# Attention and a gated two-layer network on one core: all of w_in converted before w_out, fewer weight loads queued ahead of the transposes of P, and a new plan

## The chip, the cores and the metric

The kernel runs on one core of a Trainium2 chip. The metric is the device time of one execution in microseconds (us). Before the change the median of three executions was 715.66 us (714.78 to 718.32).

## The reference, cut to what matters

```
q, k, v: (4 batches, 8 heads, 1152, 64)      x: (2304, 512)
q_pool = q.reshape(B, H, 576, 2, D).mean(axis=3)
scores = q_pool @ k.T / sqrt(D);  attn = softmax(scores);  out = attn @ v
x = out.transpose(0, 2, 1, 3).reshape(B * 576, H * D)
h = x @ w_in          # 512 x 2048
g = h * sigmoid(h)
result = g @ w_out    # 2048 x 512
```

The result is float32. All matrix products except the first scores are done as three products of float16 halves (a high part and the rest): high by high, high by low, low by high. The weights come from the host as 64-bit floats, so one weight is eight bytes, and the kernel makes the two float16 parts of each itself.

## The kernel before, in words

**Work.** The 32 heads are 16 pairs, four pairs to a batch. A job (`job`, line 731) is 128 pooled query rows of one pair: the scores S of both heads (`scores`, L723), the row maximum on VectorE (DVE, L784 and L791), the exponential on ScalarE (ACT, L800), then P cut into a high part (L816, recorded at helper lines 408 or 412) and a low part (L820, recorded at L432, mostly on GpSimd, POOL). Both parts are transposed by a DMA that SyncE (SP) issues (L827, tile `pt`), and TensorE (PE) multiplies them with V (`finish`, L935, tile `po`). In the first four jobs one of the two sides is transposed by PE instead (L841, tile `pp`). `guard` (L755) adds a small constant to the row sums and, after a reciprocal, L1007 scales `po` into x. There are 72 jobs: 64 of 128 rows of one pair, and 8 that hold the left-over 64 rows of two pairs.

**The network.** When the four jobs of 128 rows of a batch are finished, `rows` (L1017) turns x around, on PE for the first two blocks (L1064) and by DMA after that (L1044), and `block` (L1104) runs the two layers: `first(u)` for four quarters u (L1130, 48 products each, tile `mm`), tanh, gate, and the two parts of g (tile `g`, at most ten live at once by `MOST`, four to a block); then `second` (L1225, 48 products of 512 columns), which for the first block is cut into four pieces and for the second block into two (`PIECES`), each needing only a part of w_out. Quarter u of the first layer needs only the eighths 2u and 2u+1 of w_in.

**The weights.** `weights(n)` (L550) handles one of 32 pieces: an eighth u of w_in (`w1`) or w_out (`w2`), half i. It is one DMA of 512 KB (L595) and then a chain of five or six element-wise operations of 128 x 512: an ACT pass into a PSUM bank of the pool that `mm`, `po` and `pp` also use, which has two (L606); a shift on ACT or DVE (L613, L619); the two joined on DVE (L634); for w_in alone a scaling pass ("more"); the high part (`whi`); the rest (`wlo`, mostly POOL). Before, the pieces go u by u, w_in and w_out in turn:

```
        def weights(n):
            u, which, i = n // 4, n // 2 % 2, n % 2
```

The first 16 land in the space in which the second halves of the converted weights will stand later, the other 16 in the pool `b` (13 tiles in the plan), which also holds P, its parts, its transposes and the loaded q and v.

**The order.** Nothing is scheduled on the chip. `Plan.order` (L178) simulates five engines on the host with a table of costs and picks, whenever an engine is free, the ready operation of lowest priority number; the order that comes out is emitted as the program of each engine, and each engine then takes its own instructions in that order, waiting on semaphores. SP takes every load, store and transpose in one such order. Before, `departs` (L208) keeps the planner from having more than a weight of seven in flight on the DMA queue, where a transpose counts two and any other transfer one (`FLIGHT`). Priorities are sums of a job's or piece's number and a constant per kind of operation (`PRI`, `PRE` for jobs under 8, `W` for the weights, `EV` for what drains the network's products).

Of the kernel before, what the change touches and what calls it, by code (L numbers as in the profile page):

```python
# [36 lines left out]
P = 128  # L37
# [15 lines left out]

WAIT = 0.189
AHEAD, SWITCH, STEAL = 1.286, 21.317, 1.144
PREP_LEAD = 4.079
FIRST_LEAD, FIRST_STEP = 1.344, 4.504
W_FIRST, W_STEP, W2_LATER = 3.473, 0.361, -0.214
V_LATER, V_FIRST = 13.621, -45.048
PRI = dict(  # L60
    score=-258.189, top=-1.612, exp=-1.381, hi=1.631, lo=-0.034, turn=5.489, flip=13904.244,
    flat=-10.33, sums=-96.591, rows=-493.286, side=-0.32, load=-5.565, raw=0.83, xturn=-5.782,
)
PRE = dict(
    score=-0.266, top=0.223, exp=2.744, hi=1.295, lo=-1.698, turn=-0.57, sums=1.5, side=-0.268,
)
W = dict(
    t=0.374, low=0.166, put=-3777.77, more=0.289, hi=0.49, lo=-0.918,
)
EV = dict(  # L70
    x=7.188, xh=-27.052, xl=8.244, px=28.106, tanh=8.054, gate=12.388, ghi=-31.135, glo=6.951,
    osb=6.624,
)
# [16 lines left out]
FILL = {"turn": 2.79, "load": 4.6, "raw": 3.85, "store": 1.41}  # L90
MOVE = {"turn": 1.15, "load": 1.58, "raw": 1.23, "store": 0.6}
AFTER_TURN, LANDING = 0.71, 0.55
FETCH, FETCH_TIME, FETCH_STALL = 128, 1.26, 0.6
LOADS_BY, RAW_BY = "dma", "dma"
# [3 lines left out]
MORE_BY = "act", "dve", "pool"  # L98
LOW_BY = "act", "dve"
MORE = True  # L100
SUM_BY_PE = False
VC = D + 2 if SUM_BY_PE else D
X_BY_PE = 2
SIDES32 = 0
LAST = B * FULL + B // 2 - 1

# [34 lines left out]
class Plan:  # L141
# [7 lines left out]
    def add(self, options, priority, reads=(), writes=(), tiles=(), port=True, moves=None, matmuls=0, mode=0, spare=False):  # L149
        tiles = [x for t in tiles for x in (t, t.share) if x is not None]  # L150
        op = Op(options, priority, tiles, port, moves, matmuls, mode, spare)
        before = []
# [18 lines left out]
    def ready_at(self, op, engine):  # L171
        at = 0.0
        for b in op.before:
            same = b.engine == engine and engine not in ("dve", "dma")
            at = max(at, b.end + (0.0 if same else LATENCY[b.engine]))
        return at + (DMA_START if engine == "dma" else 0.0)

    def order(self):  # L178

        engines = ("pe", "dve", "act", "pool", "dma")  # L180
        free = dict.fromkeys([*engines, "port"], 0.0)
        ring, matmuls = {"dma": 0.0, "act": 0.0}, 0
        last, mode = None, 0
        flying = []
        waiting = {e: [] for e in engines}
# [21 lines left out]

        def departs(now, weight):  # L208

            landings = sorted(x for x in flying if x[0] > now)  # L210
            total = weight + sum(w for _, w in landings)
            for at, w in landings:
                if total <= FLIGHT[2] + 1e-9:
                    break
                total -= w
                now = at
            return now

        warm, used, busy, until = False, 0.0, 0.0, WINDOW
# [9 lines left out]
        def pick(e, now):  # L229
            for item in waiting[e]:  # L230
# [29 lines left out]
        while todo:  # L260
# [11 lines left out]
            while moved:  # L272
                moved = False
                for e in engines:
# [25 lines left out]
                    if op.moves:  # L300
                        what = op.moves
                        least = MOVE[what]
                        weight = FLIGHT[0] if what == "turn" else FLIGHT[1]
                        leaves = now
                        if e == "dma":
                            leaves = departs(now, weight)
                            free[e] = leaves + cost
                            if last == "turn" and what not in ("turn", "store"):
                                least += AFTER_TURN
                            last = what  # L310
                        ring[e] = max(leaves + FILL[what], ring[e] + least)
                        if e == "act" and ring["dma"] > now:
                            ring["dma"] += least
                        op.end = ring[e] + LANDING
                        if e == "dma":
                            flying = [x for x in flying if x[0] > leaves] + [(op.end, weight)]
# [44 lines left out]
def tile_kernel(tc, q, k, v, w_in, w_out, out):  # L361
    nc = tc.nc
    with ExitStack() as ctx:
# [186 lines left out]
        def weights(n):  # L550
            u, which, i = n // 4, n // 2 % 2, n % 2
            name, src, scale = (("w1", w_in, W_IN_SCALE), ("w2", w_out, W_OUT_SCALE))[which]
# [3 lines left out]
            w = wt[name, u // 4]  # L556
            if n < 16:
                space, at = n // 4, n % 4
                if at == 0:
                    wide[space] = tile("w", f"w{space % 2 + 1}_1", [P, 4, 1024], F32, "wide")  # L560
# [10 lines left out]
            t = tile("psM", "mm", [P, 512], F32)  # L571
            c = slice(i * 512, i * 512 + 512)
# [9 lines left out]

            def tu():
                return t().bitcast(U32)

            def value():
                return words(1)

            def hi():
# [7 lines left out]
                ),  # L597
                pr + PRI["raw"], writes=[("raw", *tok)], tiles=[raw], moves="raw",
            )
# [4 lines left out]
            add(  # L604
                "act", act_cost(512, True) + 0.06,
                lambda: nc.scalar.activation(  # L606
                    out=t(), in_=value(), func=AF.Prelu, scale=2.0**-111, alpha=-(2.0**32)
                ),
                pr + W["t"], [("raw", *tok)], [("t", *tok)], [t, raw], port=False,
            )  # L610
# [7 lines left out]
            def low_on(engine):  # L618
# [6 lines left out]
                "act": ("act", act_cost(512) + 0.02, low_act),  # L625
                "dve": ("dve", dve_cost(512, True), low_on(nc.vector)),
            }
            either(
                [ways[x] for x in LOW_BY],
                pr + W["low"], writes=[("low", *tok)], reads=[("raw", *tok)], tiles=[raw],  # L630
            )
            add(
                "dve", slow,
                lambda: nc.vector.scalar_tensor_tensor(  # L634
                    out=words(1).bitcast(U32), in0=tu(), scalar=3, in1=words(0).bitcast(U32),
                    op0=ALU.logical_shift_left, op1=ALU.bitwise_or,
                ),
                pr + W["put"], [("low", *tok), ("t", *tok)], [("raw", *tok)], [t, raw], port=False,
            )
            more = scale / 2.0**8  # L640
            staged = [] if n < 16 else [
                x for a in range(4) for what in ("w1", "w2") for x in weight_tokens(what, a)
            ]
# [10 lines left out]
            if more != 1.0:  # L654
                add(
                    "dve", slow,
                    lambda: nc.vector.scalar_tensor_tensor(
                        out=w()[:, u % 4, 1, c], in0=value(), scalar=more, in1=hi(),
                        op0=ALU.mult, op1=ALU.subtract,
                    ),  # L660
                    pr + W["lo"], [("raw", *tok), ("whi", *tok)], [("wlo", *tok)], [raw, w],
# [69 lines left out]
        def job(j):  # L731
# [22 lines left out]

            def guard():  # L755
                for i in range(2):
                    moves = [(slice(0, P), slice(0, P))]
# [8 lines left out]
            if SUM_BY_PE:  # L766
                return
            add(
                "dve", 0.13 if ch is not None else 0.2, guard,
                j + 0.5, [("p32", j, 0), ("p32", j, 1)], [("r", j)], [sm, r], port=False,  # L770
# [170 lines left out]
        def finish(j):  # L941
# [15 lines left out]
            for i, (pp, col) in enumerate(sides(j)):  # L957
# [7 lines left out]
                if by_32(j, i):  # L965
                    add(
                        "pe", 9 * 4 * pe_cost(64) + 0.1,
                        lambda pt=pt, pp=pp, hs=hs, keep=keep: heads(
# [363 lines left out]
```

## Time and profile before

| | |
|---|---|
| median of three executions | 715.66 us |
| the profiled execution | 714.45 us |
| its span, first to last instruction | 712.5 us |
| PE busy | 653.3 us (92%) |
| ACT, DVE, POOL busy | 480.4, 471.9, 463.9 us (67, 66, 65%) |
| mean granted PE clock | 0.976 of full |

Busy times are sums over instructions of one engine; the page's second part cuts the span into 40 slices and gives the busy share of each in tenths. PE's slices are at 4 to 8 in the first seven (about 125 us) and at 8 or 9 from there to the end.

### The profile page before, as it was taken

How to read it: one execution, taken by the hardware profiler on the slowest of the kernel's cores; microseconds unless marked ns; L12 is line 12 of the kernel's file. 1: busy time of each engine (PE TensorE's matmuls, PEld its weight loads, DVE VectorE, ACT ScalarE, POOL GpSimd, SP SyncE). 2: the span in 40 equal slices, each digit the busy share in tenths (PEclk: the TensorE clock that was granted, in tenths of full speed). 3: DMA queues.
4: the chain of work that ended last, by engine and by line, in shares of the span. 5: the costliest groups of instructions: out<-in, count | busy, mean ns of one | idle time of the engine just before them, and what ended most of it. 6: DMA issues, size and time to landing. Idle time of an engine off the chain costs nothing. (4 is left out here: it accounts for less than half of the span.)

```text
span 712.5 us, 23295 instructions
## 1 busy us (share of the span) xinstructions
PE 653.3 (92%) x10052; PEld 470.7 (66%) x10052; DVE 471.9 (66%) x839; ACT 480.4 (67%) x707; POOL 463.9 (65%) x260
## 2 busy tenths in 40 slices
PE   4656877999899999999899999998999999999997
PEld 2333655676767686767486868585868686858767
DVE  5878885689678575776678756586777565754111
ACT  4978977997577665777655766695777675865221
POOL 1657985897437776778635867887579776666111
PEclk8788999999999999999999999999999999999999
DMA  8999899999999999999999999999999999999000
GB/s 347 358 283 246 159 205 225 238 195 212 200 303 177 163 182 168 161 247 194 207 255 172 180 181 166 167 252 176 280 218 172 184 173 157 159 175 158 24 16 16
DMA packets 362886, 138.10 MB, mean 194 GB/s; under 512 B 350112, under 2 KB 350368, under 8 KB 362784
## 3 DMA queue, kind: packets, MB, share of 16 engines
q1 hardware_dynamic: 362624, 136.49, 99.6%
q8 instruction: 78, 1.28, 0.7%
q14 instruction: 24, 0.20, 0.1%
q10 hardware_dynamic: 160, 0.13, 0.1%
HBM read 45.09 MB, written 4.72 MB: 70 GB/s over the span
## 5 line engine op out<-in xcount | busy, mean ns | idle before, releaser
L432 POOL TENSOR_TENSOR phl<-p,phl 128x1152 f16<-128x1152 f32 x119 | 291.6, 2457 | 100.6 <-DVE phl L412 58.6
L800 ACT ACTIVATE p<-S,nm 128x1152 f32<-128x1152 f32 x144 | 174.8, 1215 | 99.1 <-DVE nm L791 46.5
L784 DVE TENSOR_REDUCE nm<-S 128x1 f32<-128x1152 f32 x144 | 194.5, 1351 | 53.2 <-PE S L723 52.9
L1130 PE MATMUL mm<-xt,w 128*128 128x128 f16 x3456 | 203.6, 220 | 4.8 <-DVE raw L634 2.1
L1130 PEld LDWEIGHTS <-w 128*128 128x128 f16 x3456 | 195.5, 98 | 11.1 <-DMA xt<-xs 2.5
L1225 PE MATMUL mm<-w,g 128*128 128x512 f16 x816 | 186.5, 380 | 2.1 <-DVE nm L791 1.9
L432 POOL TENSOR_TENSOR g<-t,g 128x512 f16<-128x512 f32 x72 | 98.4, 1368 | 80.4 <-ACT g L408 79.6
L723 PE MATMUL S<-K,Q 64*128 64x512 f16 (+7 forms) x1320 | 138.2, 373 | 13.4 <-ACT p L800 6.7
L935 PE MATMUL po<-V,pt 128*128 128x64 f16 (+1 forms) x4320 | 130.8, 195 | 20.0 <-DMA pt<-phl 9.8
L935 PEld LDWEIGHTS <-pt 128*128 128x128 f16 (+1 forms) x4320 | 122.3, 102 | 32.4 <-issue 12.7
L1225 PEld LDWEIGHTS <-g 128*128 128x128 f16 x816 | 75.9, 98 | 85.7 <-issue 2.5
L408 ACT ACTIVATE phl<-p 128x1152 f16<-128x1152 f32 x99 | 114.4, 1160 | 8.2 <-DMA pt<-phl 5.8
L1151 DVE SCALAR_TENSOR_TENSOR t<-t,mm 128x512 f32<-128x512 f32 x72 | 49.3, 684 | 59.8 <-ACT t L1144 57.6
L723 PEld LDWEIGHTS <-Q 64*128 64x128 f16 (+1 forms) x1080 | 42.2, 97 | 51.3 <-issue 11.1
L1144 ACT ACTIVATE t<-mm 128x512 f32<-128x512 f32 x72 | 42.5, 591 | 23.0 <-PE mm L1130 22.7
L408 ACT ACTIVATE g<-t 128x512 f16<-128x512 f32 x72 | 45.1, 627 | 18.0 <-DVE t L1151 17.9
L761 DVE TENSOR_SCALAR r<-sum 128x1 f32<-128x1 f32 (+1 forms) x152 | 17.1, 147 | 50.5 <-ACT p L800 50.1
L723 PEld LDWEIGHTS S<-K,Q 64*128 64x128 f32 (+1 forms) x240 | 23.2, 211 | 39.4 <-issue 24.2
L412 DVE CAST phl<-p 128x1152 f16<-128x1152 f32 x41 | 33.7, 822 | 9.9 <-DMA pt<-phl 7.1
L432 POOL TENSOR_TENSOR xs<-x,xs 128x512 f16<-128x512 f32 (+1 forms) x16 | 19.8, 1238 | 24.3 <-ACT xs L408 24.1
L432 DVE TENSOR_TENSOR phl<-p,phl 128x1152 f16<-128x1152 f32 x21 | 32.1, 1533 | 4.4 <-ACT phl L408 4.2
L535 DVE SCALAR_TENSOR_TENSOR V<-ld,V 128x1152 f16<-128x1152 f32 x16 | 27.6, 1729 | 6.6 <-ACT V L408 6.6
(59 smaller groups left out, 390.7 us busy)
## 6 DMA issues: line engine op xcount, KB each, us to landing
ld<-q SPq DMA_DIRECT2D x16, 576.0 KB, 5.7
ld<-v SPq DMA_DIRECT2D x16, 576.0 KB, 6.1
ld<-k SPq DMA_DIRECT2D x12, 576.0 KB, 6.4
pt<-phl SPq DMA_TRANSPOSE x280, 4.3
wide<-w_in SPq DMA_DIRECT2D x8, 512.0 KB, 8.8
wide<-w_out SPq DMA_DIRECT2D x8, 512.0 KB, 7.9
raw<-w_in SPq DMA_DIRECT2D x8, 512.0 KB, 4.9
raw<-w_out SPq DMA_DIRECT2D x8, 512.0 KB, 5.4
```

The source lines that it names most:

```text
L408: nc.scalar.activation(out=out(), in_=src(), func=AF.Copy, scale=scale or 1.0)
L412: nc.vector.tensor_copy(out=out(), in_=src())
L432: return lambda: getattr(engine, op)(out=out(), in0=a(), in1=b())
L535: lambda: nc.vector.scalar_tensor_tensor(out=values(1), in0=v3(), scalar=V_SCALE, in1=values(0)[:, :, :D], op0=ALU.mult, op1=ALU.subtract,),
L723: nc.tensor.matmul(o[to, c], lhsT=a[rows, s], rhs=x[rows, c], start=n == 0, stop=n == len(terms) - 1,)
L784: lambda: nc.vector.tensor_reduce(out=nm(), in_=ps()[:, :S], op=ALU.max, axis=AX.X),
L800: lambda: nc.scalar.activation(out=p32(), in_=ps()[:, :S], func=AF.Exp, scale=0.0625, bias=nm(), **({} if SUM_BY_PE else dict(accum_out=sm ...
L935: nc.tensor.matmul(o[to, keep : keep + n], lhsT=pt[:, hl * NK + c, cols], rhs=vv[:, at : at + n], start=c == 0 and hl + vl == 0, stop=c == ...
L1130: nc.tensor.matmul(o, lhsT=w[:, f // 2 % 4, wl, cols], rhs=moving(xl, kk), start=kk == 0 and wl + xl == 0, stop=kk == 3 and wl == 1,)
L1144: lambda: nc.scalar.activation(out=t(), in_=h(), func=AF.Tanh, scale=1.0 / G_SCALE),
L1151: lambda: nc.vector.scalar_tensor_tensor(out=t(), in0=t(), scalar=1.0, in1=h(), op0=ALU.add, op1=ALU.mult,),
L1225: nc.tensor.matmul(o(), lhsT=g[ff // 4]()[:, gl, ff % 4], rhs=w[:, u % 4, wl, e * DM : e * DM + DM], start=ff == ffs[0] and gl + wl == 0, ...
```

## The change

It does the following.

- The pieces of the weights are numbered w_in first: pieces 0 to 15 are w_in, 16 to 31 are w_out. Pieces 0 to 11 land in the space of the second halves of the converted weights or of the first half of w_out (`W_SPACES`); pieces 12 to 31, 20 instead of 16, in the pool `b`.
- In the planner `departs` and the surcharge on a load that follows a transpose are gone. Instead a weights' load is not issued while the modelled DMA queue has more than `PACE`, 5.929 us, ahead of it; a transpose holds SP's modelled queue until 0.45 us (`BACKLOG`) before the end of the transpose ahead; whatever needs a transpose is counted as ready 1.035 us (`LATE`) later than its landing; and the model of instruction fetches has other constants.
- `guard` uses one instruction for both columns of the row sums instead of two, in the 64 jobs of one pair.
- All priorities are new numbers; the plan is made anew with them.

```diff
-WAIT = 0.189
...
+WAIT = 0.233
+LATE = 1.035
...
+PREP_LEAD = 30.776
+FIRST_LEAD, FIRST_STEP = 184.155, 28.662
+W_FIRST, W_STEP, W2_LATER = -31.903, 46.348, 59.093
...
+    score=-7689049.805, top=543.78, exp=-18.862, hi=114.106, lo=-26.359, turn=1066.129,
+    flip=-951468825.963, flat=-18364455.845, sums=55234.608, rows=19917862327.894, side=-0.254,
+    load=-102.918, raw=136.844, xturn=-1240322.091,
...
+    score=-167313.439, top=-11346.633, exp=-219437.434, hi=-119435.312, lo=-264122.869,
+    turn=-755.959, sums=224665.654, side=-77.155,
...
+    t=-81.792, low=37.245, put=-86252358.206, more=34375.197, hi=-273.73, lo=164.882,
...
+W_SPACES = ("w2", 0), ("w1", 1), ("w2", 1)
...
-FLIGHT = 2, 1, 7
+BACKLOG = 0.45
+PACE = 5.929
...
-            at = max(at, b.end + (0.0 if same else LATENCY[b.engine]))
+            at = max(at, b.end + (0.0 if same else LATENCY[b.engine]) + (LATE if b.moves == "turn" else 0.0))
...
+                if e == "dma" and op.moves == "raw" and ring["dma"] > now + PACE + 1e-9:
+                    heapq.heappush(events, ring["dma"] - PACE)
+                    continue
...
+                        if what == "turn":
+                            free[e] = max(op.end, turned - BACKLOG)
+                            turned = ring[e]
...
-            u, which, i = n // 4, n // 2 % 2, n % 2
+            which, u, i = n // 16, n % 16 // 2, n % 2
...
-            if n < 16:
-                space, at = n // 4, n % 4
+            if n < 4 * len(W_SPACES):
+                space, at = W_SPACES[n // 4], n % 4
...
+                if ch is not None and by_32(j, 0) == by_32(j, 1):
+                    nc.vector.tensor_scalar(
+                        out=r(), in0=sm(), scalar1=SUM_GUARD,
+                        scalar2=1.0 / V_SCALE if by_32(j, 0) else 1.0, op0=ALU.add, op1=ALU.mult,
+                    )
+                    return
```

## Rows read from the trace of the kernel before

**Rows 1.** Windows by stage: stretch, its length, busy us (instructions) per engine, clock, DMA.
```profile
0.00:60.00 60.00, 32.83 (x270) 20.56 (x270) 44.56 (x80) 44.45 (x72) 28.32 (x25) 0.83 1.03 330
60.00:140.00 80.00, 63.95 (x886) 44.18 (x884) 59.33 (x110) 68.46 (x108) 65.35 (x41) 0.94 1.04 205
140.00:300.00 160.00, 155.64 (x2499) 113.69 (x2498) 118.36 (x203) 112.34 (x164) 108.53 (x59) 0.99 1.10 198
300.00:400.00 100.00, 94.61 (x1531) 66.78 (x1530) 72.81 (x123) 68.59 (x97) 64.36 (x35) 1.00 1.09 211
400.00:650.00 250.00, 247.38 (x4096) 179.45 (x4091) 168.06 (x311) 171.58 (x245) 181.53 (x92) 1.00 1.10 188
650.00:712.50 62.50, 58.94 (x789) 46.01 (x785) 8.83 (x14) 14.96 (x26) 15.75 (x13) 1.00 0.18 34
```

**Rows 2.** PE's waits from 0 to 140 us: us in total, times, longest.
```profile
PE pp L841 <- ACT p L800: 12.6, 4, 4.5
PE S L723 <- DMA K<-k: 6.3, 1, 6.3
PE po L935 <- DVE wide L634: 5.8, 2, 4.0
...
PE po L935 <- DMA pt<-phl: 2.0, 3, 1.0
```

**Rows 3.** PE's waits from 140 to 650 us.
```profile
PE po L935 <- DMA pt<-phl: 7.8, 13, 1.9
```

**Rows 4.** Timeline of PE: start us, us, what, count [idle before].
```profile
6.28 4.21 PE L723 MATMUL S<-K,Q 64*128 64x512 f32 x12 [6.28 <-DMA K<-k]
...
64.98 1.11 PE L1064 MATMUL px<-one,x 128*128 128x128 f32 x4 [1.84 <-DVE nm L791]
67.25 4.21 PE L723 MATMUL S<-K,Q 64*128 64x512 f32 x12 [1.15 <-ACT p L800]
...
73.14 2.85 PE L1130 MATMUL mm<-xt,w 128*128 128x128 f16 x48
75.99 2.21 PE L723 MATMUL S<-K,Q 64*128 64x512 f32 x12
...
84.41 2.21 PE L723 MATMUL S<-K,Q 64*128 64x512 f32 x12
...
92.16 2.21 PE L723 MATMUL S<-K,Q 64*128 64x512 f32 x12 [0.34 <-ACT p L800]
...
122.48 3.75 PE L723 MATMUL S<-K,Q 64*128 64x512 f32 x12 [2.20 <-ACT p L800]
```

**Rows 5.** The chain that ended last, its later part: start us, us, what.
```profile
571.37 1.68 PE po L935 x54
...
666.66 10.72 PE mm L1130 x192
677.38 10.36 PE mm L1225 x48
```

**Rows 6.** Busy DVE of line 634 alone, by stretch (the join, once per piece).
```profile
0.00:60.00 60.00, 7.58 (x12) 0.83 1.03 330
60.00:90.00 30.00, 5.01 (x8) 0.89 0.86 174
90.00:110.00 20.00, 1.96 (x3) 1.00 1.19 205
```

**Rows 7.** Timeline of SP: start us, us, what, count.
```profile
16.97 8.61 SPq L827 DMA_TRANSPOSE pt<-phl  x2
...
29.46 9.91 SPq L827 DMA_TRANSPOSE pt<-phl  x2
...
59.11 28.00 SPq L827 DMA_TRANSPOSE pt<-phl  x14
```

**Rows 8.** DMA of the first 60 us: GB/s in 40 slices of 1.5 us.
```profile
GB/s 0 166 399 412 418 412 421 418 424 414 323 366 404 426 415 421 268 297 163 384 390 379 393 363 393 186 255 154 208 369 374 372 135 348 219 390 421 393 346 154
```

**Rows 9.** Timeline of DVE: the guard, and the small operation nearest to it.
```profile
83.95 0.22 DVE L761 TENSOR_SCALAR r<-sum 128x1 f32<-128x1 f32 x2 [0.54 <-ACT p L800]
...
89.15 0.15 DVE L791 TENSOR_SCALAR nm<-nm 128x1 f32<-128x1 f32 x1
```

More of the change, by code (lines that the diff above doesn't have):

```diff
@@ L52 @@
 SUM_GUARD = 1e-9 * math.exp(P_SHIFT)
-WAIT = 0.189
[L55 to L59, printed above, removed]
+WAIT = 0.233
+LATE = 1.035
+AHEAD, SWITCH, STEAL = 1.191, 7500.906, 1.327
+PREP_LEAD = 30.776
+FIRST_LEAD, FIRST_STEP = 184.155, 28.662
+W_FIRST, W_STEP, W2_LATER = -31.903, 46.348, 59.093
+V_LATER, V_FIRST = 46260304.092, 1589936.167
 PRI = dict(
-    score=-258.189, top=-1.612, exp=-1.381, hi=1.631, lo=-0.034, turn=5.489, flip=13904.244,
-    flat=-10.33, sums=-96.591, rows=-493.286, side=-0.32, load=-5.565, raw=0.83, xturn=-5.782,
+    score=-7689049.805, top=543.78, exp=-18.862, hi=114.106, lo=-26.359, turn=1066.129,
+    flip=-951468825.963, flat=-18364455.845, sums=55234.608, rows=19917862327.894, side=-0.254,
+    load=-102.918, raw=136.844, xturn=-1240322.091,
 )
 PRE = dict(
-    score=-0.266, top=0.223, exp=2.744, hi=1.295, lo=-1.698, turn=-0.57, sums=1.5, side=-0.268,
+    score=-167313.439, top=-11346.633, exp=-219437.434, hi=-119435.312, lo=-264122.869,
+    turn=-755.959, sums=224665.654, side=-77.155,
 )
 W = dict(
-    t=0.374, low=0.166, put=-3777.77, more=0.289, hi=0.49, lo=-0.918,
+    t=-81.792, low=37.245, put=-86252358.206, more=34375.197, hi=-273.73, lo=164.882,
 )
 EV = dict(
-    x=7.188, xh=-27.052, xl=8.244, px=28.106, tanh=8.054, gate=12.388, ghi=-31.135, glo=6.951,
-    osb=6.624,
+    x=-1472.346, xh=-1738.434, xl=-56965.629, px=237092.365, tanh=-2495660.136, gate=4.509,
+    ghi=-15152.425, glo=-436.176, osb=-84.597,
 )
@@ L89 @@
 ISSUE = {"turn": 1.38, "load": 0.6, "raw": 0.6, "store": 0.6}
[L90 to L93, printed above, removed]
+FILL = {"turn": 2.87, "load": 4.23, "raw": 3.76, "store": 1.39}
+MOVE = {"turn": 0.99, "load": 1.45, "raw": 1.34, "store": 0.7}
+LANDING = 0.55
+FETCH, FETCH_LEAD, FETCH_TIME, FETCH_STALL = 128, 28, 1.24, 1.58
 LOADS_BY, RAW_BY = "dma", "dma"
@@ L150, in add @@
         tiles = [x for t in tiles for x in (t, t.share) if x is not None]
-        op = Op(options, priority, tiles, port, moves, matmuls, mode, spare)
+        op = Op(options, round(priority, 4), tiles, port, moves, matmuls, mode, spare)
         before = []
@@ L181, in order @@
         free = dict.fromkeys([*engines, "port"], 0.0)
-        ring, matmuls = {"dma": 0.0, "act": 0.0}, 0
-        last, mode = None, 0
-        flying = []
+        ring, matmuls = {"dma": 0.0, "act": 0.0}, FETCH_LEAD
+        turned, mode = 0.0, 0
         waiting = {e: [] for e in engines}
@@ L206, in shared @@
             return e == "pool" or (e == "dve" and op.port)
[L208 to L217, printed above, removed]
         warm, used, busy, until = False, 0.0, 0.0, WINDOW
@@ L301, in order @@
                         what = op.moves
[L302 to L311, printed above, removed]
+                        ring[e] = max(now + FILL[what], ring[e] + MOVE[what])
                         if e == "act" and ring["dma"] > now:
-                            ring["dma"] += least
+                            ring["dma"] += MOVE[what]
+                        if what == "turn":
+                            free[e] = max(op.end, turned - BACKLOG)
+                            turned = ring[e]
                         op.end = ring[e] + LANDING
-                        if e == "dma":
-                            flying = [x for x in flying if x[0] > leaves] + [(op.end, weight)]
                         heapq.heappush(events, free[e])
@@ L569, in bits @@
                     return raw()[:, :1024]
-            t = tile("psM", "mm", [P, 512], F32)
+            t = tile("psM", "mm", [P, 512], F32) if T_IN_PSUM else None
+            scratch = [t] if T_IN_PSUM else []
             c = slice(i * 512, i * 512 + 512)
@@ L597, in weights @@
                 ),
-                pr + PRI["raw"], writes=[("raw", *tok)], tiles=[raw], moves="raw",
+                pr + PRI["raw"], writes=[("raw", *tok), ("came", *tok)], tiles=[raw], moves="raw",
             )
             add(
-                "act", act_cost(512, True) + 0.06,
+                "act", act_cost(512, True) + 0.06 if T_IN_PSUM else 0.68,
                 lambda: nc.scalar.activation(
-                    out=t(), in_=value(), func=AF.Prelu, scale=2.0**-111, alpha=-(2.0**32)
+                    out=carried(), in_=value(), func=AF.Prelu, scale=2.0**-111, alpha=-(2.0**32)
                 ),
-                pr + W["t"], [("raw", *tok)], [("t", *tok)], [t, raw], port=False,
+                pr + W["t"], [("raw", *tok)] if T_IN_PSUM else [], [("t", *tok)] if T_IN_PSUM else [("raw", *tok), ("t", *tok)],
+                [*scratch, raw], port=False,
             )
@@ L629, in weights @@
                 [ways[x] for x in LOW_BY],
-                pr + W["low"], writes=[("low", *tok)], reads=[("raw", *tok)], tiles=[raw],
+                pr + W["low"], writes=[("low", *tok)], reads=[("raw", *tok) if T_IN_PSUM else ("came", *tok)], tiles=[raw],
             )
@@ L634, in weights @@
                 lambda: nc.vector.scalar_tensor_tensor(
-                    out=words(1).bitcast(U32), in0=tu(), scalar=3, in1=words(0).bitcast(U32),
+                    out=words(1).bitcast(U32), in0=carried().bitcast(U32), scalar=3, in1=words(0).bitcast(U32),
                     op0=ALU.logical_shift_left, op1=ALU.bitwise_or,
                 ),
-                pr + W["put"], [("low", *tok), ("t", *tok)], [("raw", *tok)], [t, raw], port=False,
+                pr + W["put"], [("low", *tok), ("t", *tok)], [("raw", *tok)], [*scratch, raw], port=not T_IN_PSUM,
             )
             more = scale / 2.0**8
-            staged = [] if n < 16 else [
-                x for a in range(4) for what in ("w1", "w2") for x in weight_tokens(what, a)
+            staged = [
+                (x, "w1", m // 2, m % 2) for at, space in enumerate(W_SPACES) if space == (name, u // 4)
+                for m in range(4 * at, 4 * at + 4) for x in ("whi", "wlo")
             ]
@@ L654, in weights, with lo_on @@
             if more != 1.0:
-                add(
-                    "dve", slow,
-                    lambda: nc.vector.scalar_tensor_tensor(
+                def lo_on(engine):
+                    return lambda: engine.scalar_tensor_tensor(
                         out=w()[:, u % 4, 1, c], in0=value(), scalar=more, in1=hi(),
                         op0=ALU.mult, op1=ALU.subtract,
-                    ),
+                    )
+                either(
+                    [x for x in (("dve", slow + 1.0, lo_on(nc.vector)), ("pool", pool_cost(512), lo_on(nc.gpsimd))) if x[0] in LO_BY],
                     pr + W["lo"], [("raw", *tok), ("whi", *tok)], [("wlo", *tok)], [raw, w],
@@ L768, in job @@
             add(
-                "dve", 0.13 if ch is not None else 0.2, guard,
+                "dve", 0.07 if ch is not None else 0.2, guard,
                 j + 0.5, [("p32", j, 0), ("p32", j, 1)], [("r", j)], [sm, r], port=False,
```

13 lines of the change are left out of this document (8 added, 5 removed).

## The prediction, made before the kernel was run

> **What bounds the kernel now.** I read the windows by stage first, because one share of busy time for the whole span hides that the limits differ. [rows 1] give PE 32.83 us busy of the first 60, 63.95 of the next 80, then 155.64 of 160, 94.61 of 100, 247.38 of 250 and 58.94 of 62.5. So PE is idle 27.2 + 16.05 = 43.2 us before 140 us and 15.9 us in the 572 us after it (4.4 + 5.4 + 2.6 + 3.6). From 140 us on the kernel is bound by PE; only the first fifth has anything large to give. The same rows show a granted clock of 0.83 and 0.94 in the first two stretches: one and the same group of twelve score products takes 4.21 us at the lower of PE's two levels, 1.2 GHz, and 2.21 us at 2.4 GHz [rows 4]; the slow groups came at the start and after stretches in which PE was mostly waiting.
>
> What holds PE in the first fifth? PE's waits there [rows 2] name the exponential of the first four jobs (12.6 us, for the transposes on PE), the first load (6.3 us) and a PSUM bank that the weights' conversion holds (5.8 us). The transposes of P by DMA stand in that list with 2.0 us only. Behind the list stand the element-wise engines: in the first 140 us DVE, ACT and POOL are busy 103.9, 112.9 and 93.7 us, 310.5 of 420 or 74%; in the second stretch 59.3, 68.5 and 65.4 of 80, with ACT at 86% [rows 1]. They convert weights and do softmax at once, so a job's scores come every 9.77 us on average over the first eight steps (84.41 - 6.28, over 8), where the step from 84.41 to 92.16 took 7.75 [rows 4]. x of the first four jobs is there only at 64.98 and the network begins at 73.14 [rows 4]; from 6 to 73 us PE has attention alone.
>
> **Part by part.** The sum is made against the profiled execution, 714.45 us; the median shown is 1.21 us above it.
>
> 1. *Attention ahead of the weights in the first eight jobs.* The new priorities put the exponential, the two parts of P and the maximum of jobs under 8 ten thousand or more below those of the conversions, the join (L634) excepted; before, conversions and jobs alternated. If the first four steps take 8.05 us, near the quickest ones seen, instead of 9.77, x of the first block and the network behind it come 4 x 1.72 = 6.9 us earlier. The conversions not done meanwhile are done later, where ACT is already at 86%, so not all of it stays. The ends are 6.9 us gained and 3 lost (the conversions of the first 60 us, twelve joins in [rows 6], pushed out by half of the 6.9 us); I take 5 us gained, because POOL is idle 31.7 of the first 60 us and DVE and ACT 15 each [rows 1].
>
> 2. *w_in first.* A block's first layer is 10.72 us of PE, its second 10.36 [rows 5]. Twelve joins were done by 60 us, 20 by 90, 23 by 110 [rows 6]. In turn order 20 pieces are five eighths of both matrices, and quarter 3 of the first layer waits for pieces 28 and 29, after 110 us. With w_in first, 16 pieces, done at about 75 us at the same pace, free all four quarters of block 0 and of block 1 as soon as its x stands; w_out begins at pieces 16 to 19, done at about 90 us, which is what the first piece of block 0's second layer needs. So some 21 us of PE work can lie between 65 and 110 us where now a quarter at a time is released. Idle there is part of the 16.05 us of the second stretch. Ends: 0 (the element-wise engines, 80% busy on average there, set the pace whatever is released) and 12 (three quarters of the idle time); I take 6. A fuller PE also meets fewer slow groups: the two at 67.25 and 122.48 us cost 2.0 and 1.5 us more than the quick one [rows 4], and I take 2 of these 3.5, with 0 and 3.5 as ends.
>
> 3. *The turns of P.* SP held two transposes for 8.61 us at 16.97 behind seven loads and for 9.91 at 29.46 behind seven, against 28.00 for fourteen, 2.0 each, at 59.11 where nothing lay ahead [rows 7]: 4.6 and 5.9 us too much. 5.929 us of modelled queue are four loads of weights at the new table's 1.34, not seven, so about three sevenths of that goes. It is hidden in the first fifth but for the 2.0 us of [rows 2]; it brings `po`, and so x, earlier, which is in 1. Later, PE waits 7.8 us for transposes in 13 places [rows 3]. The added 1.035 us makes the planner put other products in front; the longest of those waits is 1.9, the mean 0.6. Ends: 9.8 gained (all), 5 lost (an order whose other products are themselves late; half of what is there now). I take 3 gained.
>
> 4. *The guard.* Two instructions took 0.22 us, a single one on a column 0.15 [rows 9], so 0.07 less in each of 64 jobs, 4.5 us of DVE. DVE is 66% busy and behind PE after 140 us, so this is hidden by PE's products; thirteen jobs lie before, where it might show: 0 to 0.9, I take 0.5. Were PE no longer the cover, the 4.5 would count.
>
> 5. *Against it.* All twelve loads of the first four pairs now go before the first weights: the load constant for pair 3 comes to about -200 and that of piece 0 to 105, where before 6.6 stood against 4.3. Three loads of 576 KB more lie ahead, 4.1 us at the 418 GB/s that loads alone reached [rows 8]. The Trainium skill, DMA: Bandwidth & Descriptors, section "Where 436 GB/s comes from", gives about 358 GB/s as what HBM allows one core, by which it would be 4.8 us; the trace does not agree, with 412 to 424 in nine slices, and the sum would differ by well under a microsecond. Then, four more pieces use the pool `b`, and 12 pieces, not 16, can lie outside it, so P's tiles are shorter of room until w_out is through. And the scaling pass of w_in has by far the highest number of all conversions and goes last wherever something else is ready. Ends: 0 and 12 lost (worked out in the second rival); I take 3 lost.
>
> Sum: 5 + 6 + 2 + 3 + 0.5 - 3 = 13.5 us, 714.45 - 13.5 = 700.95; with the 1.2 us by which the median lies above the profiled execution, 702 us.
>
> **The rivals.**
> *The element-wise engines set the pace anyway (no change to slightly faster).* The 310.5 us of their work in the first 140 us stay but for the guard's 0.9; if they stay 74% used, x and the conversions merely change places, and only 3 to 4 us of turns and clock are left: 711 to 715 us, say 713. For it: ACT at 86% and POOL at 82% in the second stretch [rows 1]. Against: at 82% over 140 us, 310.5 / (3 x 0.82) = 126 us would do, 14 us less.
>
> *w_out too late (slower).* Ten tiles of `g` hold two and a half blocks, 26.8 us of first-layer work. From 65 us on attention takes 2.21 + 1.68 us of PE [rows 4, 5] per step of 9.77, 40%; the 26.8 us fill the other 60% for 45 us, to about 110 us. If the first four pieces of w_out (piece 20 of all) are later than that, PE idles 0.6 us for each us; before, 20 pieces took until 90 [rows 6]. If attention ahead of everything puts them off to 140, the loss is 18 us less the 8 that items 1 and 3 give: about 724 us. For it: `more` and the later pieces' numbers stand behind nearly all else, and ACT has only 14% spare where they must be done. Against: 20 us lie between 90 and 110, and POOL idles early.
>
> *PE full from the first x on.* If the network fills every gap after 55 us, all 16.05 us, the 3.5 of clock and 8 of the 20.9 us of idle time between the first score and 60 us go: 28, so 687 us. The busy ACT speaks against it.
>
> **How the numbers follow.** Forecast as summed, 694 to 709 us: 50%. Element-wise pace: 20%. w_out late: 20%. PE full: 10%. The time is the likeliest case's, 702. A measurement here tells about 0.5%, 3.6 us, from no change: faster is below 712.1, same to 719.2. Forecast and PE-full are faster (60%), of the pace case some 6 in 20: 66%; the other 14% are the same; the late case, from 720, is the slower 20%. From 688 to 720 us lie the forecast, the pace case, about half of the full case and a quarter of the late one, 80%; the ends of all items at once (20 us lost, or 33 gained) lie outside or at its edge.
>
> **What would show it.** PE busy over 0 to 140 us should rise from 96.8 towards 110 us of work (item 1 and 2), the first `px` come near 55 to 58 us, and all four quarters of block 0 follow each other before 95. The pairs of transposes that took 8.6 and 9.9 us should take under 6. PE's waits for `pt` after 140 us should halve. The clock of the first 140 us should not be lower. I am wrong if the eighth score group still starts after 80 us, if the last join of a weight piece lies well beyond 150 us with PE idle before it, or if PE's idle time after 140 us grows beyond 15.9 us, so that the new order gives back later what it gained.

## The result, and the profile after

The kernel after takes 724.98 us (median of four, 724.09 to 725.74); the ratio to the kernel before is 1.0123, with a 95% interval of 1.0095 to 1.0151. It is slower, by 9 us, where 702 us and a range of 688 to 720 were forecast. The profiled execution took 725.56 us with a span of 723.8.

The windows by stage of the kernel after answer to [rows 1]; columns are the stretch, its length, busy us of PE, PE's weight loads, DVE, ACT and POOL with instruction counts, then clock, DMA share and GB/s:

```profile
0.00:60.00 60.00, 32.30 (x270) 20.47 (x270) 42.82 (x70) 45.28 (x71) 28.86 (x28) 0.83 1.06 317
60.00:140.00 80.00, 57.79 (x767) 42.57 (x768) 63.56 (x95) 62.00 (x96) 56.46 (x38) 0.83 0.92 183
140.00:300.00 160.00, 154.77 (x2427) 109.55 (x2425) 131.10 (x189) 118.37 (x168) 110.91 (x60) 1.00 1.13 207
300.00:400.00 100.00, 96.15 (x1556) 68.89 (x1553) 88.17 (x114) 66.74 (x95) 68.59 (x38) 1.00 1.11 209
400.00:650.00 250.00, 245.71 (x3966) 177.88 (x3964) 190.70 (x276) 168.97 (x241) 164.18 (x88) 1.00 1.08 183
```

The second stretch has lost: PE is busy 57.79 us instead of 63.95, at a lower clock, so still less work was done in it. DVE, though, is busy longer in every stretch from 60 us on, with fewer instructions; over the whole span 536.8 us in 773 instructions, where it was 471.9 in 839. An engine that does fewer things and is busy 65 us longer is the row to follow. Its groups by line name the place (busy us, mean ns, idle before):

```profile
L752 DVE TENSOR_SCALAR r<-sum 128x2 f32<-128x2 f32 x64 | 75.3, 1177 | 45.8 <-ACT p L801 45.3
...
L762 DVE TENSOR_SCALAR r<-sum 64x1 f32<-64x1 f32 (+1 forms) x24 | 3.6, 149 | 5.2 <-ACT p L801 5.0
```

The guard on two columns takes 1177 ns on average, the same operation on one column 149. In [rows 9] the two one-column guards took 0.22 us together. The range within the 64 says that it isn't arithmetic (minimum, median, maximum in ns), so most of the 75.3 us is waiting, which the profile counts as busy:

```profile
L752 DVE TENSOR_SCALAR r<-sum x64: 156/1274/2360, 16.5 to 655.7; 128x2 f32<-128x2 f32 x64
```

Beside POOL's timeline it is plain what it lasts until. First DVE, then POOL, of the same stretch of the kernel after (start, length):

```profile
402.53 1.82 DVE L752 TENSOR_SCALAR r<-sum 128x2 f32<-128x2 f32 x1
404.38 0.17 DVE L774 RECIPROCAL r<-r 128x2 f32<-128x2 f32 x1
411.86 1.62 DVE L752 TENSOR_SCALAR r<-sum 128x2 f32<-128x2 f32 x1 [0.26 <-ACT p L801]
413.51 0.17 DVE L774 RECIPROCAL r<-r 128x2 f32<-128x2 f32 x1
```
```profile
401.94 2.38 POOL L422 TENSOR_TENSOR phl<-p,phl 128x1152 f16<-128x1152 f32 x1 [1.65 <-DVE phl L402]
...
411.08 2.37 POOL L422 TENSOR_TENSOR phl<-p,phl 128x1152 f16<-128x1152 f32 x1 [1.92 <-DVE phl L402]
```

402.53 + 1.82 is 404.35, and POOL's instruction ends at 404.32; 411.86 + 1.62 is 413.48 against 413.45. The guard ends when the POOL instruction that was running ends; the reciprocal behind it, also on two columns, takes 0.17 us. Counted over the whole trace, 49 of the 64 guards took more than 0.3 us, and every one of these ended 23 to 30 ns after the end of a POOL instruction; the other 15 took 156 to 171 ns. In the kernel before, 133 of the 152 one-column guards and 64 of the 72 reciprocals began while a POOL instruction was running, and none took more than 168 ns. The Trainium skill has this rule, in SBUF — State Buffer, section "SBUF: two separate sides": DVE and GpSimd share one pair of ports as an exclusive lock, held for a whole instruction, and a DVE operation wants it when it runs in a two-port mode or has two SBUF inputs (in that case only against a GpSimd operation that reads SBUF). The Trainium skill, VectorE: DVE Perf Modes, section "Mode 2×_2P — use both read ports for one tensor", puts float32 operations of one tensor and a constant into that mode, the elements split between the ports. The trace agrees: one column (149 ns), which leaves nothing to split, doesn't wait, two columns (1177) do.

The planner has such a rule too: `shared` (L205 before, L211 after) keeps what runs on POOL and every DVE operation marked `port=True` from running at once. But `guard` is marked `port=False` (L770 before, L771 after), at a modelled 0.13 us before and 0.07 after, so the plan could not see the wait. A plan made with the guard marked otherwise was not run.

How it reaches PE is seen at the turn of the first x. DVE and then PE of the kernel after:

```profile
68.93 2.32 DVE L752 TENSOR_SCALAR r<-sum 128x2 f32<-128x2 f32 x1
71.28 0.17 DVE L774 RECIPROCAL r<-r 128x2 f32<-128x2 f32 x1
71.37 0.69 DVE L626 SCALAR_TENSOR_TENSOR raw<-mm,raw 128x512 uint32<-128x512 uint32 x1
71.97 0.28 DVE L1008 TENSOR_TENSOR x<-po,r 128x128 f32<-128x128 f32 x1
72.75 1.29 DVE L626 SCALAR_TENSOR_TENSOR raw<-mm,raw 128x512 uint32<-128x512 uint32 x2 [0.50 <-ACT mm L597]
```
```profile
73.58 1.09 PE L1065 MATMUL px<-one,x 128*128 128x128 f32 x4 [5.26 <-DVE raw L626]
78.79 1.46 PE L1131 MATMUL mm<-xt,w 128*128 128x128 f16 x12 [4.12 <-DVE xt L1086]
80.18 4.21 PE L718 MATMUL S<-K,Q 64*128 64x512 f32 x12
```

The weights' joins, each of which frees a PSUM bank, stand behind the guard on DVE; PE waits 5.26 us for the bank (2.99 in the same place with two guards), then 4.12 for x's copy, and the scores after it run at the lower clock, 4.21 us where a quick group takes 2.21 [rows 4]. The chain that ended last has the guard in it, at 4.4% of the span:

```profile
by line: PE mm L1226 14.4%; PE mm L1131 12.1%; PE po L936 9.8%; issue 8.1%; PE S L718 7.8%; DVE nm L785 6.2%; DVE r L752 4.4%; ACT p L801 4.3%; DMA pt<-phl 3.6%; POOL phl L422 3.2%; DVE phl L422 2.7%; DMA wide<-w_in 1.7%; DVE t L1152 1.6%;
```

### The profile page after: what moved, and what is told of

Same layout as the page of the kernel before. It is cut to its first block, busy times and chain, and to the rows that moved or that the text cites. A ratio compares the mean times of both kernels' runs of the same rounds, so it can differ in the third digit from the quotient of the medians.

```text
span 723.8 us, 23224 instructions
## 1 busy us (share of the span) xinstructions
PE 656.3 (91%) x10052; PEld 475.2 (66%) x10052; DVE 536.8 (74%) x773; ACT 485.9 (67%) x705; POOL 452.7 (63%) x264
## 4 chain that ended last, share of the span: by engine, by line
PE 46%; DVE 22%; DMA 10%; ACT 8%; issue 8%; POOL 4%; SPq 1%; DVEq 0%; ACTq 0%; POOLq 0%
PE mm L1226 14%; PE mm L1131 12%; PE po L936 10%; PE S L718 8%; DVE nm L785 6%; DVE r L752 4%; ACT p L801 4%; DMA pt<-phl 4%; POOL phl L422 3%; DVE phl L422 3%; DMA wide<-w_in 2%; DVE t L1152 2%; PE mm L1179 1%; DMA ld<-k 1%; DMA raw<-w_out 1%
## 5 line engine op out<-in xcount | busy, mean ns | idle before, releaser
L422 POOL TENSOR_TENSOR phl<-p,phl 128x1152 f16<-128x1152 f32 x115 | 279.1, 2434 | 130.6 <-ACT phl L398 71.9
L1131 PE MATMUL mm<-xt,w 128*128 128x128 f16 x3456 | 206.5, 221 | 7.6 <-DVE xt L1086 4.1
L1131 PEld LDWEIGHTS <-w 128*128 128x128 f16 x3456 | 197.8, 99 | 14.0 <-DVE xt L1086 4.5
L422 POOL TENSOR_TENSOR g<-t,g 128x512 f16<-128x512 f32 x71 | 94.1, 1325 | 77.6 <-ACT g L398 62.4
L398 ACT ACTIVATE phl<-p 128x1152 f16<-128x1152 f32 x106 | 122.4, 1161 | 2.3 <-DMA pt<-phl 0.2
L752 DVE TENSOR_SCALAR r<-sum 128x2 f32<-128x2 f32 x64 | 75.3, 1177 | 45.8 <-ACT p L801 45.3
L422 DVE TENSOR_TENSOR phl<-p,phl 128x1152 f16<-128x1152 f32 x25 | 41.8, 1674 | 2.2 <-ACT phl L398 1.9
L1008 DVE TENSOR_TENSOR x<-po,r 128x128 f32<-128x128 f32 x72 | 20.6, 286 | 21.8 <-PE po L936 19.8
L422 POOL TENSOR_TENSOR xs<-x,xs 128x512 f16<-128x512 f32 (+1 forms) x18 | 23.3, 1294 | 19.7 <-ACT xs L398 17.7
L398 ACT ACTIVATE V<-ld 128x1152 f16<-128x1152 f32 x15 | 17.3, 1157 | 23.1 <-DMA ld<-v 23.1
```

Of the source, the lines that this page charges most:

```text
L398: nc.scalar.activation(out=out(), in_=src(), func=AF.Copy, scale=scale or 1.0)
L422: return lambda: getattr(engine, op)(out=out(), in0=a(), in1=b())
L752: nc.vector.tensor_scalar(out=r(), in0=sm(), scalar1=SUM_GUARD, scalar2=1.0 / V_SCALE if by_32(j, 0) else 1.0, op0=ALU.add, op1=ALU.mult,)
L1008: lambda: nc.vector.tensor_tensor(out=to(), in0=sides2()[:, :, :D], in1=r().unsqueeze(2).to_broadcast([P, 2, D]), op=ALU.mult,),
L1131: nc.tensor.matmul(o, lhsT=w[:, f // 2 % 4, wl, cols], rhs=moving(xl, kk), start=kk == 0 and wl + xl == 0, stop=kk == 3 and wl == 1,)
```

## The experiments

Ratios are to the kernel before, run beside them on the same chip, with 95% intervals.

**The guard, both ways.** The kernel after with two guards, and the kernel before with one (the same lines, added); the orders of all engines stay.

```diff
-                if ch is not None and by_32(j, 0) == by_32(j, 1):
-                    nc.vector.tensor_scalar(
-                        out=r(), in0=sm(), scalar1=SUM_GUARD,
-                        scalar2=1.0 / V_SCALE if by_32(j, 0) else 1.0, op0=ALU.add, op1=ALU.mult,
-                    )
-                    return
```

> The kernel after, in the same planned order, with the guard as two one-column instructions per job again. In the kernel after the one two-column guard takes 1177 ns on average (75.3 us in 64) where the two of before took 0.22 us together. Theory G (the guard is the cause: it waits for POOL and DVE's later work waits behind it): the 60 us of DVE go, and nearly all of the 9.3 us lost come back, 714 to 717 us. Theory O (the order of the first 140 us is the cause: the guards before 140 us cost only some 4 us together, and after 160 us PE idles no more than before): 721 to 724 us.

715.95 us, 1.0031 (1.0003 to 1.0058).

> The kernel before, in the same planned order, with the one two-column guard. Theory G: the guard takes about 1.1 us here too, DVE is busy some 55 to 60 us longer, and the time rises by most of the 9.3 us, to 721 to 725 us. Theory O: the guard is as long, but PE hides it; at most 4 us slower, 715 to 719 us. If the guard's length does not come from the instruction but from the new plan, it takes 0.15 us here and nothing changes.

724.18 us, 1.0130 (1.0093 to 1.0168). The one instruction, put into the kernel before, costs as much as the whole change did: 1.3% of 714 us is 9.3 us. Its row, and PE's waits of that run after 140 us, beside those of [rows 3]:

```profile
L757 DVE TENSOR_SCALAR r<-sum 128x2 f32<-128x2 f32 x64 | 74.9, 1170 | 44.9 <-ACT p L806 44.6
```
```profile
PE po L941 <- DMA pt<-phl: 5.9, 10, 1.7
PE po L941 <- DVE t L1157: 4.6, 8, 1.3
PE po L941 <- DVE nm L797: 3.0, 1, 3.0
```

The waits for DVE are new or longer (1.2 us for the gate's `t` before): the gate is the last to read a bank that `po` then takes. So here most of the loss does not lie at the first x but later: from 140 to 650 us PE is busy 488.91 us, against 497.63 in [rows 1], and before 140 us 95.28 against 96.78. Taken out of the kernel after, the guard gives back 0.92% (1.0123 to 1.0031), some 6.6 us. Theory G holds; theory O, which gave the early guards 4 us and the rest to the order, is refuted for most of the loss.

**The same cost in another form.** Two columns, but an addition of two SBUF tensors.

```diff
+        tiny = tile("tiny", "tiny", [P, 2], F32)
...
+                if ch is not None:
+                    nc.vector.tensor_tensor(out=r(), in0=sm(), in1=tiny(), op=ALU.add)
+                    return
```

> The kernel before, in the same planned order, with the guard as one two-column addition of two SBUF tensors (the sums and a constant tile) instead of one tensor with an immediate. If the long guard is a matter of the second read path that DVE shares with POOL, which an operation on two SBUF inputs also needs: about 1.1 us each again, 720 to 725 us. If it belongs to the tensor-with-immediate form alone: 0.15 to 0.2 us each, 713 to 716 us.

721.77 us, 1.0117 (1.0071 to 1.0164), and the row:

```profile
L761 DVE TENSOR_TENSOR r<-sum,tiny 128x2 f32<-128x2 f32 x64 | 73.7, 1152 | 44.9 <-ACT p L807 44.5
```

1152 ns against 1170: the form with an immediate is not needed for the wait. These guards too end with POOL: the 47 that took more than 0.3 us ended 14 to 22 ns after the end of a POOL instruction. That the two forms wait for the same shared ports is the rule named above; the runs show only that both wait for POOL, and that one column and the reciprocal do not.

**No guard at all**, the reciprocal reading the sums in the 64 jobs.

```diff
+                if ch is not None:
+                    nc.vector.reciprocal(out=r(), in_=sm())
+                    return
...
-                "dve", 0.08, lambda: nc.vector.reciprocal(out=r(), in_=r()),
+                "dve", 0.08, lambda: None if ch is not None else nc.vector.reciprocal(out=r(), in_=r()),
```

> The kernel before, in the same planned order, with the guard left out in the 64 jobs of one pair: the reciprocal reads the sums directly, so the added 6.4e-8 (against sums of 63 and more) is left out there. DVE is spared 64 x 0.21 = 13 us. If DVE's small work on the way to x costs PE anything in this order, as theory G has it for the long guard: 709 to 712 us before's 713.8. If only a long DVE wait hurts and short work is hidden: no change, within 2 us.

715.38 us, 1.0009 (0.9992 to 1.0025): 13 us less of DVE work in short pieces change nothing that can be measured.

> The kernel after, in the same planned order, without the guard in the 64 jobs of one pair (the 6.4e-8 is left out). Theory G: all of the guard's 75 us go and the time is that of two guards or 1 to 3 us less, 712 to 716 us. It tells what the new order is worth with the least guard there can be: if it still isn't below before without a guard, the new order gives nothing.

716.32 us, 1.0019 (1.0002 to 1.0036). Without a guard in either, the two orders differ by 0.1%, inside the intervals. So the new order gains nothing, where the prediction summed 13 us for it.

**Parts of the order.** First the numbering of the weights alone, w_in first under the old priorities and in turn under the new ones:

```diff
-            u, which, i = n // 4, n // 2 % 2, n % 2
+            which, u, i = n // 16, n % 16 // 2, n % 2
...
```

The second run has the same edit the other way round, and the long guard still in it.

> The kernel before with all its priorities and its planner, and only the pieces of the weights renumbered, w_in first and w_out last, with the three spaces for 12 pieces. Theory O in its form that the order of the weights costs: 720 to 726 us. Theory O in its form that the priorities and the pacing cost, or theory G: 712 to 718 us. The prediction's own step (w_in first gives about 6 us): 708 to 711 us.

720.11 us, 1.0081 (1.0053 to 1.0108).

> The kernel after with its priorities, planner and one guard, and the pieces of the weights in turn again, u by u, with the four spaces for 16 pieces. The priorities were not made for this numbering. If w_out last is what costs: 715 to 720 us. If the priorities and the pacing cost, or the guard: 723 to 732 us.

739.49 us, 1.0365 (1.0317 to 1.0414).

Then single constants of the kernel after with two guards: `rows=-493.286`, `T_IN_PSUM = False`, `PACE = 1e9`, `LATE = 0.0`.

> The kernel after with two guards, and the priority of turning x on PE as it was before (first of all instead of last of all), planned anew. With two guards x of the first four jobs was turned at 70.3 us, after before's 65.0, though the eighth scores came 7.5 us earlier. If x being turned late holds the network back: the turn comes near 60 us and the time falls by 2 to 5 us below that of two guards. If the weights' conversion and the PSUM banks hold it: no change within 3 us.

733.56 us, 1.0272 (1.0252 to 1.0291). x was turned from 64.05 us on, 6.3 us earlier (near 60 was expected), and the time went the other way. This expectation sets the eighth score group with two guards, 76.91, against the ninth of before, 84.41; the eighth of before began at 75.99 [rows 4], so those scores were not 7.5 us earlier but 0.9 later.

> The kernel after with two guards, and the conversion's intermediate kept in SBUF in place (the switch T_IN_PSUM off), planned anew, so that no weight piece holds one of the two PSUM banks of po, mm and px. PE waits for those banks some 16 us in the first 140 us with two guards (lines 930, 1059 behind line 626). If that wait holds back the first stage: 3 to 8 us faster. Against it: the pass on ACT and the join then wait for each other's data in place, and the join reads SBUF twice, so that it may wait for POOL like the guard: 0.69 us become 1.2 or more in 32 joins, and 0 to 10 us slower.

758.75 us, 1.0627 (1.0610 to 1.0645). The last join of a weight piece came at 251.6 us; PE waited 26.0 us in the first 140 for the exponential before scores. The join now has two SBUF inputs: ten of the 32 began behind a running POOL instruction, took 0.83 to 1.65 us and ended 0.52 to 0.55 after it; the others took 0.68 to 0.70.

> The kernel after with two guards, and no pacing of the weights' loads (PACE without limit), planned anew. If few loads ahead of the turns of P is worth what the prediction gave it (part of 3 us): 717 to 720 us. If it is hidden, no change beyond what a plan made anew moves. The last join of a weight piece is to be read beside the time.

745.04 us, 1.0454 (1.0398 to 1.0509); last join at 200.0 us.

> The kernel after with two guards, and nothing added to the landing of a transpose in the planner (LATE 0), planned anew. PE's waits for pt after 140 us, 7.8 us before and 0.5 us with two guards, should come back to 4 us and more if LATE is what removed them, and the time rise by 2 to 6 us; if pacing removed them they stay under 2 us.

732.00 us, 1.0260 (1.0214 to 1.0307); waits for `pt` after 140 us were 6.3 us.

**What a plan made anew is worth by itself.** The first of these gives the very same order on every engine, so it is a repeat of two guards:

> The kernel after with two guards, and one planner constant (WAIT) at 0.234 instead of 0.233, planned anew. Nothing about the machine is different; it shows how far a plan made anew moves the time for no reason. Any value within 3 us of 716 would let single runs with a changed constant be read; a change of 8 us or more would say that their differences up to that size mean nothing by themselves.

716.88 us, 1.0030 (0.9997 to 1.0063), against 1.0031. The next three do give other orders:

```diff
-    return 0.06 + n * (0.00053 if fast else 0.00105)
+    return 0.061 + n * (0.00053 if fast else 0.00105)
```

> The kernel after with two guards, and the planner's fixed cost of a DVE operation at 0.061 us instead of 0.060; this does give another order on every engine. If a plan made anew from nearly the same costs lands within 3 us of 716, the losses of the runs without pacing (745), without the added landing (732) and with x at once (734) come from those constants. If it lands 10 us and more away, those runs only show that the priorities fit one plan, and their constants are not told apart from that.

734.82 us, 1.0267 (1.0237 to 1.0298).

> The kernel before with the same 0.001 us on the planner's DVE cost, which gives another order on every engine. If before's plan is as much a single find as after's: 720 to 735 us. If its small priorities make it steadier: 712 to 717 us.

722.49 us, 1.0106 (1.0066 to 1.0146).

> The kernel after with two guards, and LATE at 0.935 instead of 1.035, planned anew. If LATE itself is what costs when it is gone (18 us in all), a tenth of it should cost 1 to 3 us: 716 to 719 us. If it is any other plan that costs: 10 us and more.

740.26 us, 1.0335 (1.0296 to 1.0374): a tenth of `LATE` costs more than all of it.

A thousandth of a microsecond in one planner cost loses 1.1% in the kernel before and, from 1.0031, 2.4% in the kernel after. So the losses of the runs with the turn of x, `LATE` and the numbering (0.8 to 3.7%, the largest with the long guard in it) are of the size that other orders cost, and say nothing of those constants. The two largest, without pacing and with the intermediate in SBUF, lie above the three such runs there are; that is too few to call their causes shown. Late conversion goes with some of these losses but is not the common cause: the last join was at 160.2 us with two guards and at 161.4 in the run of 734.82, which loses its time later instead:

```profile
140.00:300.00 160.00, 154.95 (x2424) 109.36 (x2424) 119.68 (x207) 115.91 (x165) 108.58 (x60) 1.00 1.16 210
300.00:650.00 350.00, 344.81 (x5666) 249.68 (x5664) 239.98 (x427) 239.28 (x341) 243.75 (x126) 1.00 1.11 191
```
```profile
140.00:300.00 160.00, 151.75 (x2319) 107.52 (x2317) 112.39 (x197) 110.10 (x159) 106.30 (x56) 0.99 1.08 198
300.00:650.00 350.00, 337.27 (x5424) 242.37 (x5423) 233.17 (x418) 240.61 (x340) 222.89 (x119) 0.99 1.07 189
```

Two guards first, then the run with 0.061: 5.2 us idle from 300 to 650 us against 12.7. No kernel that was run beats the kernel before.

## Why the prediction was wrong, step by step

Against the 702 us that were forecast the kernel after is some 22 us late (1.0123 against 0.981 of before): 6.6 of these come with the guard, which took the time out of the range, and the other 16 stay with two guards, where the order should have gained 13 us and gained nothing. So two steps failed, the price of the guard and the gain of items 1 and 2.

**Item 4, the guard, failed outright.** It was put at 0.5 us gained, with 0 and 0.9 as ends, by the one-column row nearest to it [rows 9]; measured, it costs 6.6 us in the kernel after and 9.3 in the kernel before. The error was to take a row of another form as the bound of an operation that the trace did not show: a two-column operation with an immediate is a different form, and the nearest rows of that kind stood in the trace. They are the shifts of the weights (L619, one tensor and a constant), of the kernel before in the first 140 us:

```profile
L619 DVE TENSOR_SCALAR raw<-raw 128x512 uint32<-128x512 uint32 x4 | 5.0, 1265 | 0.0
...
L619 DVE TENSOR_SCALAR wide<-wide 128x512 uint32<-128x512 uint32 x8 | 3.7, 482 | 0.2 <-DMA wide<-w_out 0.2
```

One and the same operation took 1265 ns on average in one group and 482 in the other. That spread was the sign. The cover named for it, PE's products, held for most of the time but not for all: 61 us more of DVE cost 9.3. PE's banks are drained by DVE and there are two of them, so what showed, by the waits above, is where a late DVE kept PE from a bank.

**Item 1, attention first, failed too.** The 84.41 us of [rows 4], eight steps from the first scores, is the start of the ninth group. The ninth began at 92.75 in the kernel after and at 89.18 with two guards, where the step makes it 77.5 (84.41 less 6.9). The kernel with two guards:

```profile
46.07 2.21 PE L718 MATMUL S<-K,Q 64*128 64x512 f32 x12
...
76.91 3.55 PE L718 MATMUL S<-K,Q 64*128 64x512 f32 x12
...
89.18 2.21 PE L718 MATMUL S<-K,Q 64*128 64x512 f32 x12
...
105.52 0.82 PE L1220 MATMUL mm<-w,g 128*128 128x512 f16 x3 [1.46 <-DVE raw L626]
...
114.42 0.64 PE L1059 MATMUL px<-one,x 128*128 128x128 f32 x4
```

The first four steps took 10.26 us each in the kernel after and 9.94 with two guards. The prediction had 8.05, from 9.77, a mean over eight steps; the first four alone took 10.92 before. So there was a gain, 3.9 us at the fifth group (46.07 against 49.97), and it was gone at the eighth (76.91 against 75.99). The fourth part of x was written at 64.37 us instead of 64.90, and x was turned at 73.58 (70.3 with two guards) instead of 64.98: it stood behind the weights' joins for a PSUM bank, a wait which the prediction had read in [rows 2] and then left out of the step. From 60 to 140 us PE waited for banks behind the joins for 12.9 us in the kernel after and 9.7 with two guards, against 5.0 before. The network began at 78.79 (75.51) instead of 73.14, and x of the second block was turned at 114.42 with two guards, 98.73 before.

**Item 2, w_in first, is wrong as a gain.** With two guards PE did 288 products of the first layer by 140 us instead of 240, and 24 of the second instead of 51:

```profile
L1125 PE MATMUL mm<-xt,w 128*128 128x128 f16 x288 | 18.0, 224 | 4.9 <-DVE xt L1080 4.1 <-DVE nm L786 0.8
...
L1220 PE MATMUL mm<-w,g 128*128 128x512 f16 x24 | 6.0, 380 | 1.8 <-DVE raw L626 1.5 <-DVE x L1002 0.4
```
```profile
L1130 PE MATMUL mm<-xt,w 128*128 128x128 f16 x240 | 14.7, 220 | 2.5 <-DVE raw L634 2.1 <-DVE x L1007 0.4
...
L1225 PE MATMUL mm<-w,g 128*128 128x512 f16 x51 | 12.2, 379 | 2.1 <-DVE nm L791 1.9 <-DVE t L1151 0.3
```

The first fence is the kernel after with two guards, the second the kernel before, both to 140 us: 24.0 us of the network against 26.9. The prediction counted in its sum what w_in first releases and left what w_out last withholds to a rival: the second layer began at 105.52 us, where before its first pieces ran at 81.73. Sixteen joins, as many as w_in needs, had begun by 70.07 with two guards, so w_in was early, as forecast. But PE needed from 75.51 to 104.05 for the four quarters of block 0, which were to be through before 95, with attention and the waits for banks between them; and the first piece of the second layer is planned behind four pieces of w_out, and SP issued the fourth load only at 86.02, so that the twentieth join began at 100.46, where about 90 was forecast:

```profile
86.02 3.55 SPq L586 DMA_DIRECT2D raw<-w_out  x5
```

The reading of [rows 6] has an error in it as well: a join that runs across the end of a stretch is counted in both, so 19 joins, not 20, had begun by 90 us before, and the twentieth began at 95.69. What put the load so late in SP's order, priorities, room in the pool `b` or pacing, is not shown. The 2 us for the clock went the same way: 0.87 in the second stretch with two guards, 0.94 before.

**Item 3, the turns, came as a shorter wait.** PE's waits for `pt` from 140 to 650 us fell from 7.8 us [rows 3] to 0.9, where 3 us were taken. Waits of other kinds took their place, so that PE's idle time in that stretch is 13.4 us in the kernel after, against 12.4 before:

```profile
PE S L718 <- ACT p L801: 4.5, 4, 2.5
...
PE po L936 <- DMA pt<-phl: 0.9, 3, 0.5
```

With two guards they are 3.8 and 0.5 us, and the idle time is 10.2, 2.2 less than before. That `LATE` or the pacing did it is not shown, since the runs without them have other orders throughout.

**Item 5 and the rivals.** The first join began at 24.64 us instead of 19.00, so the three loads ahead showed (they are 4.2 us at 418 GB/s, not 4.1). "w_out too late" gave 724 us, next to what was measured, and that is luck in the number: half of its mechanism was there, w_out's fourth piece came 10 us later than the sum had it (14 in the kernel after, 104.04), but PE had not run out of first-layer work by 140 us (288 products with two guards, where the ten tiles of `g` hold 480), and the 6.6 us that took the time to 724 are the guard's. The guard was no rival, though the change named it. "The element-wise engines set the pace anyway", 711 to 715 us, is nearest to the kernel after with its guard two again: 715.95, or 0.3% more than before instead of a small gain. There PE idles 46.6 us before 140 us and 14.2 after, against 43.2 and 15.9 before, so the order gains later what it loses earlier. Two of the three signs of being wrong came in the kernel after: the eighth score group began at 80.18 us, though the eighth of before, at 75.99, would have passed that test, and PE's idle time after 140 us was 17.6 us. The last join began at 164.5, 11 us after that of the kernel before (153.38).

## What to carry to other kernels

When an edit fuses small DVE operations, ask what form comes out: in this kernel two columns on SBUF with an immediate, or two SBUF inputs, waited for whatever GpSimd was doing, one column did not, and at 64 places this was worth 1%. When steps of two kernels are compared, count the same job in both: the eighth group with the eighth. An order that was found by search is a single find: judge a change to such a kernel by edits that leave the order of every engine as it is, and measure first how far a meaningless change of a cost moves the time.

## What the runs showed of the hardware that had not been expected

A DVE instruction on 256 values took 156 to 2360 ns, by what POOL was doing, while the reciprocal of the same shape took 149 to 167 in all 72 places. Leaving out 13 us of DVE work in pieces of 0.15 us changed the time by 0.09% (-0.08 to 0.25), and adding 61 us (74.9 against the 13.6 of the one-column guards of the same jobs) in pieces of 1.2 us by 1.3%. In proportion to the 61 us, the 13 us would be 0.28%, just outside that interval. This fits a reading in which the length of a single stall in front of PSUM's draining counts, and not DVE's share, but it is weak and not shown; a run with fewer and longer stalls was not made.
